# Splitting batch 0 of a Sinkhorn attention over both partition halves

## The chip, the cores and the metric

The kernel runs on one core of a Trainium2 chip. The metric is the device time of one execution in microseconds, as the median of three runs.

## The reference

Four batches, 8 heads, 768 positions, head size 64. The positions form 8 blocks of 96. A small matrix `sort_net` (8 x 8 for each batch and head) is normalised five times over rows and columns after an exponential, and its result P mixes the blocks of keys and values. Each block of queries then attends only to the mixed block of the same number. The result, 3072 tokens of 512, goes through a gated FFN of width 1536.

```python
P = sort_net
for _ in range(5):
    P = np.exp(P - np.max(P, axis=-1, keepdims=True))
    P = P / (np.sum(P, axis=-1, keepdims=True) + 1e-09)
    P = P / (np.sum(P, axis=-2, keepdims=True) + 1e-09)
k_sorted = np.einsum('bhij,bhjcd->bhicd', P, k_b)
v_sorted = np.einsum('bhij,bhjcd->bhicd', P, v_b)
scores = scale * np.matmul(q_b, k_sb.transpose(0, 1, 2, 4, 3))
attn = softmax(scores)                       # over the 96 keys of the block
x = np.matmul(attn, v_sb)                    # then tokens x (heads * 64)
g = x @ w_gate
out = (g / (1 + np.exp(-g)) * (x @ w_val)) @ w_out
```

## The kernel before

**Batches and units.** Every batch is split into 8 units. In the kernel before, a unit is four blocks of one pair of heads: `half, g = divmod(u, 4)`, heads 2g and 2g+1, blocks half*4 to half*4+3. A unit goes through scores (`scores`), the exponential on ScalarE (`exps`), the product with the mixed values (`av`: matmuls, then a reciprocal and a multiplication on VectorE into the tile `st`), and a transposition into `xt`, the FFN's input of 128 x 4 x 384. Four units fill one `xt`, which is one of eight FFN stages (`ffn(0)` to `ffn(7)`).

**The FFN.** `gate` and `value` are groups of four matmuls of 384 columns (L355, L373), followed by a tanh on ScalarE (L363) and two operations on VectorE (L365, L378). `outp` multiplies by the last weights (L390). `merge` lays the units of the next batch and its mixing between the FFN groups by fixed due times. From the first FFN stage on, TensorE and GpSimd run an order written out by hand, and the other engines follow.

**The opening.** Everything ahead of the first FFN stage is an order written by hand on TensorE, GpSimd, VectorE and ScalarE (`manual_schedule`). The parts are these.

- SyncE issues the load of `sort_net` into `p_sb` and nothing else until the first outputs. GpSimd's queue issues, in this order, two halves of v (batch 0), the identity, q, four pieces of k, then three transposing copies of v into `vch` (L124), a copy `landed` that waits for the last piece of k (L144), and the weights. The loads from GpSimd's queue cast fp32 to bf16 on the way.
- VectorE clears tiles (L70 to L163; L163 writes the column of ones of `vt`, 128 elements with a step of 65), then runs the five normalisations in turn with ScalarE's exponentials (L184 to L200). In iteration 1 it also makes the 0/1 `mask` (L187) and copies the identity into `rmix` (L188). The result is `p_bf` (L203).
- ScalarE makes four more copies of v into `vch` between its exponentials (L122).
- TensorE runs small matmuls on zeros (`dots`, `fill`, L420 and L416) in its gaps. Then it transposes P (`w_ps`, L432), and VectorE multiplies it by the mask into `rmix` (L439), a block-diagonal matrix over (head, block).
- Mixing: `v_chunk` multiplies pieces of `vch` (64 partitions) by `rmix` (L245), `kq_chunk` does the same for k and q together (L233). For this the tile `kq0` holds k on the lower 64 partitions and q on the upper 64, and `rmix` holds P below and the identity above, so that one matmul mixes k and transposes q. Each chunk is drained from PSUM by VectorE (L211) or ScalarE (L213).
- The first four units (`qk`, `av`, `x_to`) follow, with the first three FFN groups (`early`, L497) laid in where their inputs are ready. PSUM has two pairs of banks (tags a and b), three single banks (gen) and one more (x).

Of the kernel before, what the change touches and what calls it, by code (L numbers as in the profile page):

```python
# [9 lines left out]
FP32 = mybir.dt.float32  # L10
# [7 lines left out]
def kernel(  # L18
# [59 lines left out]
    e_all = const.tile([C, 8, 4 * C + 32], BF16)  # L78
# [12 lines left out]
    def load_k(b, lo, hi):  # L91
        rows = highr if b else lowr
        nc.gpsimd.dma_start(out=kq_tile(b)[rows, lo:hi, :], in_=k_nat[b, :, lo:hi, :])
# [6 lines left out]
    def load_q(b, lo, hi):  # L100
        rows = lowr if b else highr
        nc.gpsimd.dma_start(out=kq_tile(b)[rows, lo:hi, :], in_=q_nat[b, :, lo:hi, :])
# [31 lines left out]
    load_v(0, 0, HC)  # L134
    load_v(0, HC, C)
    make_identity(nc, ident)
    load_q(0, 0, C)
    for lo, hi in ((0, 32), (32, 64), (64, 80), (80, 96)):
        load_k(0, lo, hi)
    copy_v(nc.gpsimd, 0, lowr, 0)  # L140
    copy_v(nc.gpsimd, 0, lowr, 3)
    copy_v(nc.gpsimd, 0, lowr, 5, 8, 40, D)
    landed = const.tile([R, 1], BF16)
    nc.gpsimd.tensor_copy(landed, kq_tiles[0][0:R, C - 1, D - 1:D])  # L144
    for m in range(0, 1024, 256):
        load_gv(m, m + 256)
    load_v(1, 0, C)
    for m in range(1024, DF, 256):
        load_gv(m, m + 256)
# [5 lines left out]
    for t in rmix.values():  # L155
        nc.vector.memset(t, 0.0)
# [3 lines left out]
    def vt_tile(pair):  # L160
        if pair not in vts:
            t = vtp.tile([C, 2, H * NB, D + 1], BF16, name=f"vt{pair}", tag="vt")
            nc.vector.memset(t[:, :, :, D:D + 1].rearrange("p u n e -> p (u n) e"), 1.0)  # L163
            vts[pair] = t
        return vts[pair]
# [4 lines left out]
    mask = const.tile([128, H], BF16)  # L170
    id4 = ident.rearrange("p (u h j) -> p h u j", u=2, h=H)
# [10 lines left out]
    p_ps = bank_tile("p_ps")[0:BH, 0:NB * NB].rearrange("p (i j) -> p i j", j=NB)  # L182
    for it in range(N_ITER):
        nc.scalar.activation(p_ps, p_sb if it == 0 else p_ps, AF.Exp)  # L184
        if it == 1:
            with nc.allow_low_precision("0/1 mask"):
                nc.vector.tensor_reduce(mask, id4, axis=AX.XY, op=ALU.add)  # L187
            nc.vector.tensor_copy(rmix[0][highr, 1].rearrange("p h i -> p (h i)"), ident[highr, highr])  # L188
        if it == 2:
            copy_v(nc.scalar, 0, lowr, 2, 8)  # L190
        if it == 3:
            copy_v(nc.scalar, 0, lowr, 3, 8)
        rowred = rowreds[it]
        nc.vector.reduce_sum(rowred[:, :, 0], p_ps, axis=AX.X)
        nc.vector.reciprocal(rowred, rowred)
        nc.vector.tensor_mul(p_ps, p_ps, rowred.to_broadcast([BH, NB, NB]))
        nc.vector.reduce_sum(colred[:, 0, :], p_ps.transpose([0, 2, 1]), axis=AX.X)
        nc.vector.reciprocal(colred, colred)
        if it < N_ITER - 1:
            nc.vector.tensor_mul(p_ps, p_ps, colred.to_broadcast([BH, NB, NB]))  # L200
    for lo in (0, NB // 2):
        part = slice(lo, lo + NB // 2)
        nc.vector.tensor_tensor(  # L203
            p_bf[:, part], p_ps[:, part].unsqueeze(2).to_broadcast([BH, NB // 2, H, NB]),
            colred.unsqueeze(1).to_broadcast([BH, NB // 2, H, NB]), op=ALU.mult)
    copy_v(nc.scalar, 0, lowr, 4, 8)
    copy_v(nc.scalar, 0, lowr, 5, 8, 0, 40)

# [6 lines left out]
    kqts = {}  # L215
# [22 lines left out]
    def v_chunk(b, at, n, eng, tag):  # L238
        rows = slice(0, 128) if b % 2 else lowr
        dst = vt_tile(b // 2)[:, b % 2]  # L240
# [8 lines left out]
    def v_pair_chunk(pair, at, n, eng, tag):  # L249
        dst = vt_tile(pair)[:, :, :, at:at + n]  # L250
# [8 lines left out]

    es, sts, xts = {}, {}, {}  # L260
    ecount = [0]

    def scores(b, u, tag):
        half, g = divmod(u, H2)
        k_sb, k_at, q_sb, q_at = ((kqts[b], 0, kqts[b], GI * C) if b < 2 else
                                  (kqts["p"], (b - 2) * GI * C, kqts["q"], (b - 2) * GI * C))
        if tag == "gen":
            wide = None
            pss = [bank_tile("qk"), bank_tile("qk")]
        else:  # L270
            wide = pair_tile("qk", tag).rearrange("p (two n) -> p two n", two=2)
            pss = [wide[:, 0], wide[:, 1]]
        for i4 in range(4):
            at = (g * NB + half * 4 + i4) * C
            for two in range(2):
                lo = two * D
                nc.tensor.matmul(pss[two][:, i4 * C:(i4 + 1) * C],  # L277
                                 lhsT=k_sb[lo:lo + D, k_at + at:k_at + at + 128],
                                 rhs=q_sb[lo:lo + D, q_at + at:q_at + at + C],
                                 start=True, stop=True)  # L280
        return wide, pss

    def exps(b, u, wide, pss):
        n = ecount[0] % 8
        ecount[0] += 2
        if wide is None:
            for two in range(2):
                nc.scalar.activation(e_all[:, n + two, 0:4 * C], pss[two][0:C, 0:4 * C], AF.Exp, scale=scale)
        else:
            nc.scalar.activation(e_all[:, n:n + 2, 0:4 * C], wide[0:C, :, 0:4 * C], AF.Exp, scale=scale)  # L290
        es[(b, u)] = [e_all[:, n, :], e_all[:, n + 1, :]]
# [4 lines left out]
    def av(b, u, tag="a"):  # L296
        half, g = divmod(u, H2)
        vt = vts[b // 2][:, b % 2].rearrange("p (h i) e -> p h i e", h=H)
        av_ps = pair_tile("av_ps", tag).rearrange("p (two n) -> p two n", two=2)
        o = av_ps[:, :, 0:4 * (D + 1)].rearrange("p two (i e) -> p two i e", e=D + 1)  # L300
        for two in range(2):
            e = es[(b, u)][two]
            for i4 in range(4):
                nc.tensor.matmul(o[:, two, i4, :], lhsT=e[:, i4 * C:i4 * C + 128],  # L304
                                 rhs=vt[:, 2 * g + two, half * 4 + i4, :],
# [106 lines left out]
    idle_ps = bank_tile("idle_ps", "x")  # L412

    def fill(tile, n):
        for _ in range(n):
            nc.tensor.matmul(tile, lhsT=warm_sb[:, 0:128], rhs=warm_sb, start=True, stop=True)  # L416

    def dots(n):
        for _ in range(n):
            nc.tensor.matmul(idle_ps[0:32, 0:32], lhsT=warm_sb[:, 0:32], rhs=warm_sb[:, 0:32],  # L420
                             start=True, stop=True)

    dots(124)
    for it, n in ((1, 3), (2, 4), (3, 4), (4, 4)):
        nc.tensor.matmul(idle_ps[0:NB, 0:NB], lhsT=rowreds[it][:, :, 0], rhs=rowreds[it][:, :, 0],
                         start=True, stop=True)
        fill(idle_ps, n)

    def weights(half):
        w_ps = bank_tile(f"w_ps{half}")[:, 0:NB * B * H].rearrange("p (i b h) -> p i b h", b=B, h=H)  # L430
        for i in range(NB):
            nc.tensor.matmul(w_ps[half * R:(half + 1) * R, i].rearrange("p b h -> p (b h)"),  # L432
                             lhsT=p_bf[:, i].rearrange("p a b -> p (a b)"),
                             rhs=ident[0:BH, 0:BH], start=True, stop=True)
        return w_ps

    def mix_of(dst, b, w):
        lo = (b % 2) * R
        nc.vector.tensor_tensor(dst, mask[lo:lo + R].unsqueeze(2).to_broadcast([R, H, NB]),  # L439
                                w[lo:lo + R].transpose([0, 2, 1]), op=ALU.mult)  # L440

    w_lo = weights(0)
    mix_of(rmix[0][lowr, 0], 0, w_lo[:, :, 0])
    w_hi = weights(1)
    w_sb = const.tile([128, NB, 2, H], FP32)
    nc.scalar.copy(w_sb[lowr, :, 1], w_lo[lowr, :, 2])
# [182 lines left out]
```

## Time and profile before

| | us |
|---|---|
| span of the profiled execution | 248.0 |
| median of the three runs | 249.75 (249.3 to 249.91) |
| TensorE busy | 240.1 |
| VectorE busy | 157.7 |
| ScalarE busy | 110.3 |
| GpSimd busy | 52.5 |

The page gives the span of the profiled execution, from its first to its last instruction; 1.75 us lie between it and the median of the runs. Busy time is the time in which an engine has an instruction at work; on TensorE matmuls overlap, so its rows may sum to more than the time that passes. In the timelines each line is a group of like instructions: start, time from the start of the first to the end of the last, engine, line, operation, tiles and shapes, and in brackets the idle time ahead of it and what ended it.

### The profile page before, as it was taken

The numbers are of one execution on the slowest core, as the hardware profiler recorded it, in microseconds if no ns is written. First come the engines' busy times: TensorE is split into PE (matmuls) and PEld (weight loads), VectorE is DVE, ScalarE is ACT, GpSimd is POOL, SyncE is SP. The second block draws the span as 40 slices with busy tenths as digits, with TensorE's granted clock in tenths as the row PEclk, the third lists the DMA queues.
The fourth block names the chain that finished last, engine by engine and source line by source line (L and its number), as shares of the span: only waits on it lengthen the run. The fifth ranks groups of instructions, "written<-read, shape, count | busy, mean of one in ns | idle before, by whom it ended". The sixth has DMA issues, their size and how long they took to land.

```text
span 248.0 us, 6193 instructions
## 1 busy us (share of the span) xinstructions
PE 240.1 (97%) x2636; PEld 141.3 (57%) x2636; DVE 157.7 (64%) x332; ACT 110.3 (44%) x187; POOL 52.5 (21%) x47
## 2 busy tenths in 40 slices
PE   7899999999999999999999999999999999999994
PEld 6376566666555556655555655565555555555543
DVE  6778689887555775857657646755764585446700
ACT  2977553453544444454642552354244334232311
POOL 7948459960059200000000000000000000000000
PEclk9999999999999999999999999999999999999999
DMA  5959999999999296010122121112111121100122
GB/s 101 211 95 166 215 189 228 194 226 211 221 170 192 53 210 164 3 42 3 45 54 52 57 62 34 44 42 78 32 42 45 39 57 55 42 22 24 42 81 88
DMA packets 39530, 24.38 MB, mean 98 GB/s; under 512 B 27728, under 2 KB 35664, under 8 KB 38992
## 3 DMA queue, kind: packets, MB, share of 16 engines
q0 software_dynamic: 21328, 14.16, 38.9%
q1 hardware_dynamic: 18176, 9.84, 14.1%
q8 instruction: 20, 0.33, 0.5%
q14 instruction: 6, 0.05, 0.1%
HBM read 28.32 MB, written 7.86 MB: 146 GB/s over the span
## 4 chain that ended last, share of the span: by engine, by line
PE 83%; DVE 7%; ACT 3%; issue 3%; DMA 2%; DVEq 0%; ACTq 0%; POOLq 0%
PE v_ps L373 23%; PE o_ps L390 23%; PE g_ps L355 22%; PE tkq L233 4%; PE av_ps L304 3%; PE qk L277 2%; DVE gs_sb L365 2%; DMA v<-in_v_dram 2%; DVE st L310 2%; PE tv L245 2%; PE idle_ps L416 1%; DVE h L378 1%; PE o_ps L406 1%; ACT th_sb L363 1%; PE x_ps L321 1%
## 5 line engine op out<-in xcount | busy, mean ns | idle before, releaser
L365 DVE SCALAR_TENSOR_TENSOR gs_sb<-th_sb,g_ps 128x384 bf16<-128x384 bf16 x96 | 52.8, 550 | 51.8 <-ACT th_sb L363 49.1
L373 PE MATMUL v_ps<-xt,wv_sb 128*128 128x384 bf16 x380 | 77.3, 326 | 0.7 <-DVE gs_sb L365 0.4
L355 PE MATMUL g_ps<-xt,wg_sb 128*128 128x384 bf16 x376 | 76.5, 326 | 0.0
L363 ACT ACTIVATE th_sb<-g_ps 128x384 bf16<-128x384 f32 x96 | 47.1, 490 | 56.0 <-PE g_ps L355 53.5
L390 PE MATMUL o_ps<-wo_sb,h 128*128 128x512 bf16 x276 | 64.0, 379 | 0.0
L378 DVE SCALAR_TENSOR_TENSOR h<-v_ps,gs_sb 128x384 bf16<-128x384 f32 x96 | 53.3, 556 | 6.6
L373 PEld LDWEIGHTS <-wv_sb 128*128 128x128 bf16 x380 | 35.4, 97 | 24.6 <-issue 2.3
L355 PEld LDWEIGHTS <-wg_sb 128*128 128x128 bf16 x376 | 34.6, 97 | 23.2 <-issue 0.3
L390 PEld LDWEIGHTS <-h 128*128 128x128 bf16 x276 | 26.3, 98 | 28.9
L395 ACT COPY o_sb<-o_ps 128x512 f32<-128x512 f32 x23 | 13.5, 585 | 50.8 <-PE o_ps L390 50.8
L124 POOL COPY vch<-v 64x1536 bf16<-64x1536 bf16 (+2 forms) x11 | 28.6, 2639 | 20.7 <-DMA v<-in_v_dram 20.7
L290 ACT ACTIVATE e_all<-qk 96x768 bf16<-96x768 f32 x30 | 22.6, 802 | 8.1 <-PE qk L277 8.1
L310 DVE TENSOR_TENSOR st<-av_ps,r_sb 96x512 bf16<-96x512 f32 x32 | 21.7, 679 | 0.2
L304 PEld LDWEIGHTS <-e_all 96*128 96x128 bf16 x256 | 12.2, 98 | 4.9 <-ACT e_all L290 0.8
L304 PE MATMUL av_ps<-vt,e_all 96*128 96x65 bf16 x256 | 13.5, 194 | 0.0
L211 DVE CAST vt<-tv 96x1024 bf16<-96x1024 f32 (+1 forms) x9 | 9.8, 1100 | 2.7 <-PE tv L255 1.6
L308 DVE RECIPROCAL r_sb<-av_ps 96x8 f32<-96x8 f32 x32 | 6.4, 199 | 7.6 <-PE av_ps L304 7.5
L213 ACT CAST vt<-tv 96x1024 bf16<-96x1024 f32 (+1 forms) x9 | 9.2, 1032 | 3.1 <-PE tv L255 1.8
L211 DVE CAST kqt<-tkq 128x1024 bf16<-128x1024 f32 (+1 forms) x7 | 7.5, 1068 | 2.7 <-PE tkq L233 2.6
L213 ACT CAST kqt<-tkq 128x1024 bf16<-128x1024 f32 (+1 forms) x7 | 6.0, 894 | 6.6 <-PE tkq L233 6.6
L416 PE MATMUL idle_ps<-warm_sb 128*128 128x512 bf16 x28 | 8.7, 409 | 0.0
L233 PE MATMUL tkq<-rmix,kq 128*64 128x64 bf16 x384 | 7.8, 197 | 0.6 <-issue 0.6
(74 smaller groups left out, 126.3 us busy)
## 6 DMA issues: line engine op xcount, KB each, us to landing
out_dram<-o_sb SPq DMA_DIRECT2D x23, 256.0 KB, 2.0
v<-in_v_dram POOLq DMA_DIRECT2D x3, 768.0 KB, 19.9
kq<-in_q_dram POOLq DMA_DIRECT2D x2, 768.0 KB, 13.6
wg_sb<-in_moe_w_gate_dram POOLq DMA_DIRECT2D x6, 256.0 KB, 8.5
wv_sb<-in_moe_w_val_dram POOLq DMA_DIRECT2D x6, 256.0 KB, 9.1
wo_sb<-in_moe_w_out_dram POOLq DMA_DIRECT2D x1, 1536.0 KB, 23.8
kp<-in_k_dram POOLq DMA_DIRECT2D x2, 768.0 KB, 15.1
q_scr<-in_q_dram POOLq DMA_DIRECT2D x2, 768.0 KB, 29.9
```

Of the source, the lines that this page charges most:

```text
L124: eng.tensor_copy(dst, src.transpose([0, 2, 1]))
L211: nc.vector.tensor_copy(dst, src)
L233: nc.tensor.matmul(tp[two * D:(two + 1) * D, lc, :], lhsT=kq_tiles[b][:, at + lc, :], rhs=rm[:, two], start=True, stop=True)
L290: nc.scalar.activation(e_all[:, n:n + 2, 0:4 * C], wide[0:C, :, 0:4 * C], AF.Exp, scale=scale)
L304: nc.tensor.matmul(o[:, two, i4, :], lhsT=e[:, i4 * C:i4 * C + 128], rhs=vt[:, 2 * g + two, half * 4 + i4, :], start=True, stop=True)
L310: nc.vector.tensor_tensor(st.rearrange("p i two d -> p two i d"), o[0:C, :, :, 0:D], r_sb.to_broadcast([C, 2, 4, D]), op=ALU.mult)
L355: nc.tensor.matmul(g_ps, lhsT=wg_sb[:, kc, ts(m, 128)], rhs=xt[:, kc, :], start=(kc == 0), stop=(kc == NKC - 1))
L363: nc.scalar.activation(th_sb, g_ps, AF.Tanh, scale=0.5)
L365: nc.vector.scalar_tensor_tensor(gs_sb, th_sb, 1.0, g_ps, op0=ALU.add, op1=ALU.mult)
L373: nc.tensor.matmul(v_ps, lhsT=wv_sb[:, kc, ts(m, 128)], rhs=xt[:, kc, :], start=(kc == 0), stop=(kc == NKC - 1))
L378: nc.vector.scalar_tensor_tensor(h_tiles[n][:, m, :], v_ps, 0.5, gs_tiles.pop(m), op0=ALU.mult, op1=ALU.mult)
L390: nc.tensor.matmul(o_ps, lhsT=h_w[:, m, ts(t3, 128)], rhs=wo_sb[:, m, :], start=(m == 0), stop=(m == NFC - 1))
```

## The change

It touches the opening and, for the units of batch 0, the shapes.

- Values of batch 0 are loaded by SyncE in four pieces, as fp32, into a tile `v0` whose lower 64 partitions hold positions 0 to 47 of each block and whose upper 64 hold positions 48 to 95. Four transposing copies over 128 partitions (three on GpSimd, one on ScalarE) cast them into `vch0`.
- q and k of batch 0 are split over the partition halves in the same way, in the tile `qk0`: four loads of q, then six of k, all from GpSimd's queue. q is transposed by matmuls of its own (`q0_chunk`) against the identity; half of them run between the fourth and the fifth normalisation, the rest after the first value chunk. k is mixed by `k0_chunk`, values by `v0_chunk`, whose two halves take 64 partitions each.
- The mixed keys lie in `kqt0` with 128 columns for a block (two times 48 and 16 of zeros), so scores, exponentials and `av` of batch 0 work on 128 keys of which 32 are padding. The padding of `vt` has zeros, in the column of ones too; that column is written by five memsets for the two pairs of batches.
- `rmix[0]` is made by one operation over 128 partitions; the mask is made in iteration 2 and has 16 columns; the copy of the identity into `rmix[0]` is gone. The operations that make `rmix` of the other batches move from ahead of the first scores to behind `av` of unit 1.
- `landed` is gone. Memsets of padding on GpSimd are new.
- The first four units of batch 0 are two blocks of four heads each; `x_first` writes half of the columns of two parts of `xt`, and `early` runs the first three FFN groups in two halves of 192 columns, the first half after two units.
- Several `fill` calls are gone or moved.

```diff
-    load_v(0, 0, HC)
-    load_v(0, HC, C)
+    v0 = vnp.tile([128, HC, D], FP32, name="v0", tag="vn")
+    for lo, hi in ((0, 24), (24, HC)):
+        for a, rows in enumerate(halves):
+            nc.sync.dma_start(out=v0[rows, lo:hi, :], in_=v_nat[0, :, a * HC + lo:a * HC + hi, :])
+    load_qk0(0, q_nat, 0, 24)
+    load_qk0(0, q_nat, 24, HC)
     make_identity(nc, ident)
-    load_q(0, 0, C)
-    for lo, hi in ((0, 32), (32, 64), (64, 80), (80, 96)):
-        load_k(0, lo, hi)
-    copy_v(nc.gpsimd, 0, lowr, 0)
-    copy_v(nc.gpsimd, 0, lowr, 3)
-    copy_v(nc.gpsimd, 0, lowr, 5, 8, 40, D)
-    landed = const.tile([R, 1], BF16)
-    nc.gpsimd.tensor_copy(landed, kq_tiles[0][0:R, C - 1, D - 1:D])
+    nc.gpsimd.memset(vch0[:, :, HC:], 0.0)
+    load_qk0(1, k_nat, 0, 16)
+    load_qk0(1, k_nat, 16, 32)
+    load_qk0(1, k_nat, 32, HC)
+    copy_v0(nc.gpsimd, 0, 24, 32, D)
+    copy_v0(nc.gpsimd, 24, HC, 0, 32)
+    copy_v0(nc.gpsimd, 24, HC, 32, D)
+    nc.gpsimd.memset(kqt0[:, 0:NK].rearrange("p (n c) -> p n c", c=D)[:, :, HC:], 0.0)
     for m in range(0, 1024, 256):
         load_gv(m, m + 256)
     load_v(1, 0, C)
+    nc.gpsimd.memset(vch[lowr, D * D:D * C], 0.0)
...
-            nc.vector.memset(t[:, :, :, D:D + 1].rearrange("p u n e -> p (u n) e"), 1.0)
+            if pair == 0:
+                nc.vector.memset(ones[:, 0], 0.0)
+                for lo in (0, R):
+                    nc.vector.memset(ones[lo:lo + HC, 0], 1.0)
+                nc.vector.memset(ones[0:C, 1], 1.0)
+            else:
+                nc.vector.memset(ones[0:C], 1.0)
...
+    def q0_chunk(at, n, tag):
+        dst = kqt0[:, NK:].rearrange("p (n a c) -> p a n c", a=2, c=HC)
+        sel = ident.rearrange("p (a g two j) -> p two (a g) j", a=2, g=H2, two=2)
+        tp = chunk_tile("tq0", n // 8, tag).rearrange("p (l n) -> p l n", n=2 * GI)
+        for lc in range(n):
+            for two in range(2):
+                nc.tensor.matmul(tp[two * D:(two + 1) * D, lc, :], lhsT=qk0[:, 0, at + lc, :],
+                                 rhs=sel[:, two], start=True, stop=True)
+        return dst[:, :, :, at:at + n], tp.rearrange("p l (a n) -> p a n l", a=2)
+    def v0_chunk(at, n, eng, tag):
+        tp = chunk_tile("tv0", n // 8, tag).rearrange("p (l n) -> p l n", n=H * NB)
+        for ld in range(n):
+            for a, rows in enumerate(halves):
+                nc.tensor.matmul(tp[rows, ld, :], lhsT=vch0[rows, at + ld, :],
+                                 rhs=rmix[0][rows, a].rearrange("p h i -> p (h i)"),
+                                 start=True, stop=True)
+        drain(eng, vts[0][:, 0, :, at:at + n], tp.transpose([0, 2, 1]))
...
-            nc.vector.tensor_copy(rmix[0][highr, 1].rearrange("p h i -> p (h i)"), ident[highr, highr])
+        if it == 3:
+            copy_v0(nc.scalar, 0, 24, 0, 32)
+        if it == N_ITER - 2:
+            early_q = [q0_chunk(0, 16, "b"), q0_chunk(16, 8, "gen")]
+        if it == N_ITER - 1:
+            for dst, src in early_q:
+                drain("s", dst, src)
...
+    v0_chunk(0, 16, "v", "a")
+    q_late = [q0_chunk(24 + 8 * n, 8, "gen") for n in range(3)]
+    for dst, src in q_late:
+        drain("s", dst, src)
+    v0_chunk(16, 16, "v", "b")
+    nc.scalar.copy(w_sb[lowr, :, 1], w_ps[lowr, :, 2])
+    nc.scalar.copy(w_sb[highr], w_ps[highr].rearrange("p i (pair u) h -> p i pair u h", u=2)[:, :, :, 1])
+    k0_chunk(0, 8, "s", "gen")
+    k0_chunk(8, 8, "s", "gen")
+    v0_chunk(32, 16, "v", "a")
+    v0_chunk(48, 16, "s", "b")
+    k0_chunk(16, 8, "s", "gen")
+    k0_chunk(24, 8, "v", "gen")
+    k0_chunk(32, 8, "s", "gen")
+    k0_chunk(40, 8, "v", "gen")
+    fill(idle_ps, 3)
     qk(0, 0, "a")
     qk(0, 1, "b")
     qk(0, 2, "gen")
     fill(idle_ps, 2)
     av(0, 0, "a")
     fill(idle_ps, 2)
     av(0, 1, "b")
+    for b in range(1, B):
+        mix_of(...)
+    x_first(0, "s", "x")
+    qk(0, 3, "a")
+    av(0, 2, "b")
+    x_first(1, "s", "gen")
+    early(0, range(NKC), 0)
+    av(0, 3, "a")
+    early(1, range(NKC), 0)
+    x_first(2, "s", "x")
+    early(2, range(NKC), 0)
+    x_first(3, "v", "x")
+    for n in range(3):
+        early(n, range(NKC), 1)
```

## The prediction

> **What bounds the kernel now.** I read the page first (engine totals, the slices), then the timelines of the first 30 us engine by engine, because the change touches nothing later.
>
> ```profile
> span 248.0 us, 6193 instructions
> PE 240.1 (97%) x2636; PEld 141.3 (57%) x2636; DVE 157.7 (64%) x332; ACT 110.3 (44%) x187; POOL 52.5 (21%) x47
> PE 83%; DVE 7%; ACT 3%; issue 3%; DMA 2%; DVEq 0%; ACTq 0%; POOLq 0%
> ```
>
> TensorE is busy for 97% of the span and carries 83% of the chain of waits: from the first full FFN matmul on, the kernel is a stream of matmuls. A change of the opening moves the end by as much as it moves the start of that stream. I call the start F. The TensorE timeline gives four marks:
>
> ```profile
> 12.30 2.04 PE L245 MATMUL tv<-rmix,vch 64*128 64x64 bf16 x64
> 14.27 2.16 PE L233 MATMUL tkq<-rmix,kq 128*64 128x64 bf16 x112
> 20.24 0.69 PE L277 MATMUL qk<-kqt 64*128 64x96 bf16 x24
> 27.24 0.81 PE L373 MATMUL v_ps<-xt,wv_sb 128*128 128x384 bf16 x4
> ```
>
> T = 12.30, block mixing starts; Q = 20.24, first scores; F = 27.24. So mixing takes 7.94 us and the first units 7.00 us. What stands ahead of T is seen on VectorE and GpSimd:
>
> ```profile
> 1.94 0.17 DVE L163 MEMSET vt<- 96x128 bf16 x1 [0.41 <-issue]
> 2.51 0.17 DVE L163 MEMSET vt<- 96x128 bf16 x1 [0.41 <-issue]
> 2.65 0.21 DVE L194 TENSOR_REDUCE rowred<-p_ps 32x8 f32<-32x64 f32 x1
> 4.26 0.32 DVE L188 COPY rmix<-ident 64x64 bf16<-64x64 bf16 x1
> 4.61 0.21 DVE L194 TENSOR_REDUCE rowred<-p_ps 32x8 f32<-32x64 f32 x1
> ```
> ```profile
> 1.27 1.19 POOL L108 DMA_DIRECT2D v<-in_v_dram  x2 [0.82 <-POOLq L613]
> 6.30 6.18 POOL L124 COPY vch<-v 64x1536 bf16<-64x1536 bf16 x3 [0.70 <-DMA v<-in_v_dram]
> 15.94 0.18 POOL L144 COPY landed<-kq 64x1 bf16<-64x1 bf16 x1 [3.45 <-DMA kq<-in_k_dram]
> ```
>
> Each strided memset of vt comes after 0.41 us in which VectorE stands still for no semaphore. The two v issues on GpSimd take 652 and 547 ns, so they end at about 1.92 and 2.46, just before the memsets at 1.94 and 2.51 start. I read that as the memset being held until a descriptor issue ends. Values land at 6.25 and k at 15.94; T waits for neither, only for the normalisation.
>
> **The change, part by part.**
>
> *Normalisation (ahead of T).* The rmix COPY goes and the mask reduction moves to iteration 2. The exp of iteration 1 ended at 4.28, its reduction began at 4.61, elsewhere 0.03 after the exp: gain 0.30 us. Against it stand five strided vt memsets for two, beside four q issues in a row on GpSimd (about 1.27 to 3.5 at 0.53 to 0.65 each). If none is held, they take 384 elements at 0.17 us per 128, end by 2.0 and cost nothing, as the first exp ends at 2.62. If one goes into each gap (1.94, 2.51, 3.03, 3.55, 3.62), the first reduction starts at 3.75, 1.1 us late. The short ones have half the elements and may pass in twos, which gives 3.25. I take 0.9, near the case that the rows show. Sum for this path: +0.6, T at 12.9.
>
> The Trainium skill, "VectorE: DVE Perf Modes", section "Zero memsets can be issued as uint32 (trn2)", says that a memset takes one cycle per element. By that alone the five cost nothing here and T would be 12.0; the start-to-start distance of the two rows, 0.57 us for 128 elements, contradicts it, and the row decides.
>
> *Values (ahead of T).* They leave the GpSimd queue for SyncE's, four issues behind the one for sort_net (0.40 us each by that row: 0.75 to 2.75; that queue has nothing else to issue before the outputs at 62.9), and land as fp32, beside q on the other queue. Between 4 and 14 us the windows show 182 to 242 GB/s written as bf16, so about 200 written and 400 read. v and q are 3.15 MB to read and now 2.36 MB to write. If reading limits: 3.15/0.4 = 7.9 us from 2.2, v whole at 10.1. If writing into a 64-partition half limits: 2.36/0.2 = 11.8 us, v whole at 14.0. No row shows a plain fp32 load into half of the partitions; I take the middle, 12.0. Then GpSimd's second copy must run (768 elements for 1536: from the rows of 653 ns for 288 and 2829 for 1536, 1.74 ns an element plus 0.15, so 1.5 us), since the first value chunk reads it: T at 13.5, between 11.6 and 15.5. It is later than 12.9 and decides: T +1.2. ScalarE's one copy (1.5 us by its 64x768 rows) sits ahead of the last exp, where 1.5 us are free; it costs nothing if the first v quarters land by 8.
>
> The Trainium skill, "DMA: Bandwidth & Descriptors", section "Rules for kernel authors", speaks against the split: two transfers to the two partition halves serialize, one over 128 partitions is better. "SBUF — State Buffer", section "Door 1: The DMA port swizzle (why `[64,N]` ≈ `[32,N]`)", gives 196 GB/s for 64 partitions; estimated from it, v's 1.57 MB alone take 8.0 us. Read-limited loads would leave T at 12.9, serialized halves put it at 15.5.
>
> *GpSimd's queue.* The last k third (two issues, about 1.1 us) now waits for q's first quarters; behind it stand three value copies, a pad memset and all weight loads. The k and q pad memsets (1024 elements each; ident's 128 took 0.25) cost about 1.3 each. Weights start at 13.5 + 1.5 + 1.3 = 16.3 instead of 16.06. Nothing: the first weight is read at 25.0. That cover of 5 us gone, each us is a us of F. k moves after q and v: 1.57 MB at 400 GB/s from 12.0 is whole at 16, and its last third is read 4.5 after T, at 18.0; no wait. The vch memset later (2048 elements, 2.5 us) stands behind eight queued loads and costs nothing.
>
> *Mixing, T to Q.* The 24 early q rows leave this stretch (48 of 192 matmuls at 18 ns and 1536 of 10240 drained elements), and so do three fills of 0.32 and the 0.57 us issue gap, while the values' matmuls double to 128. TensorE needs 2.3 + 0.9 + 1.7 = 4.9 us and no longer sets the pace; the drains do. By this kernel's rows (DVE 1024 elements 1.22, 512 0.68; ACT 1.06 and 0.60) ScalarE has 3 q drains, w_sb twice, 4 k and 1 v: 5.4 us starting 0.95 after T. The last k chunk waits for a bank until 5.75, is multiplied at 6.15 and drained at 6.85. So 6.9 for 7.94: gain 1.0, between 0.6 and 1.5.
>
> *First units, Q to F.* As before, VectorE ends st of unit 0 at Q+2.64 and of unit 1 at Q+3.48. Then the three mix rows (0.26 + 0.54), which lay beside the wait for Q, stand in its queue and unit 2's reciprocal waits behind them: to 4.28, st done at 5.2. Unit 3's scores wait for unit 0's bank, its exp ends on ScalarE at 4.3 and x_first(1)'s drain behind it at 4.75; TensorE in order then does half of early(0), av(0,3) at 4.97, reciprocal 5.43, st 6.36, transposes 6.4 to 6.74, drain 7.13, and ten matmuls of 192 columns at 0.08: F = Q+8.0. Before it was 7.0. Half-width FFN work fills waits, but the last st is 1.05 later (25.55 is Q+5.31). Cost +1.0, between +0.4 and +1.2.
>
> Sum: +1.2 − 1.0 + 1.0 = +1.2 on F. The page gives a span of 248.0 and the runs a median of 249.75; I keep the 1.75 between them. Predicted: 250.9 us.
>
> **The rivals.**
>
> *Faster.* Loads are limited by what is read. Then v is whole at 10.1, its copies end at 11.6 and T goes with the normalisation, at 12.0 if the memsets pass freely. With mixing at 6.4 and a tail of 7.4, F = 25.8 to 26.4: about −1.1, 248.6. For it: 365 GB/s written in the half microsecond at 7.0, when v and q fill both halves. It decides if v lands before 10.5 and the first reduction starts by 2.9.
>
> *Cancelled.* The same loads but held memsets: T at 12.7, mixing 6.9, tail 7.8, F = 27.4: 249.9.
>
> *Much slower.* Writes to one half at a time limit: v whole at 14.0, T at 15.5, Q 22.4, F = 30.1 to 30.4: +2.9, 252.7. For it: the steady 200 GB/s written into one half. It decides from a landing after 13.
>
> **How the numbers follow.** Forecast 0.40, faster 0.28, cancelled 0.14, much slower 0.18. About 0.3%, 0.75 us, is what this measurement can tell. Of the forecast's 0.40, 0.07 lies within that, as a v landing 0.4 us earlier brings it there. So faster 0.28, same 0.21, slower 0.51. The range runs from 248.4 (the faster case, a little further) to 252.7, leaving out the tails beyond both. The forecast's own range is 250.2 to 251.8.
>
> **What would show it.** Right: vt memsets spread to 3 us and beyond; the first tv0 matmul waiting for GpSimd's copy, near 13.5; the last k drain 6.9 after it; three mix rows between st of units 1 and 2; the first L452 row near 28.4. Wrong: v landed by 10, T near 12, or L452 before 27.

## The result and the profile after

The changed kernel takes 261.27 us (median of 4 runs, 258.64 to 261.33) against 249.83 us before (249.3 to 249.93). The ratio is 1.0423, with a 95% interval of 1.0371 to 1.0475. The prediction of 250.9 us and its range up to 252.7 us are both missed; the sign of the forecast is right, its size is not. The profiled execution took 261.33 us, 1.77 us more than its span.

The same lines of the page as before:

```profile
span 259.6 us, 6353 instructions
PE 243.4 (94%) x2706; PEld 144.3 (56%) x2706; DVE 156.8 (60%) x331; ACT 107.3 (41%) x187; POOL 55.6 (21%) x52
...
PEclk9988799999999999999999999999999999999999
...
PE 79%; DVE 6%; DMA 5%; issue 3%; ACT 3%; SPq 1%; POOL 1%; DVEq 0%; ACTq 0%; POOLq 0%
```

TensorE is busy for 3.3 us more in a span 11.6 us longer, so most of the loss is standing still. DMA now has 5% of the chain (2% before), and the granted clock, which was at its full value in every slice before, dips in slices 3 to 5. TensorE's timeline gives the three marks and two stops:

```profile
17.42 1.06 PE L284 MATMUL tv<-rmix,vch 64*64 64x64 bf16 x32 [2.46 <-POOL vch L157]
24.53 0.32 PE L276 MATMUL tk<-rmix,qk 128*64 128x64 bf16 x9 [0.74 <-ACT kqt L213]
26.86 0.29 PE L276 MATMUL tk<-rmix,qk 128*64 128x64 bf16 x7 [2.01 <-issue]
28.03 1.14 PE L356 MATMUL qk<-kqt 64*128 64x96 bf16 x24
37.05 0.81 PE L452 MATMUL v_ps<-xt,wv_sb 128*128 128x384 bf16 x4
```

T is 17.42, Q is 28.03, F is 37.05. T waits for GpSimd's value copy, as forecast, but four microseconds later. In the middle of the last key chunk TensorE stops for 2.01 us with no semaphore to wait for ("issue"). The sum by stretches, in us:

| stretch | before | after | difference | predicted difference |
|---|---|---|---|---|
| start to T | 12.30 | 17.42 | +5.12 | +1.2 |
| T to Q | 7.94 | 10.61 | +2.67 | −1.0 |
| Q to F | 7.00 | 9.02 | +2.02 | +1.0 |
| F to the end of the span | 220.76 | 222.51 | +1.75 | 0 |
| span | 248.00 | 259.56 | +11.56 | +1.2 |

What holds T is read on GpSimd and ScalarE:

```profile
10.22 0.51 POOL L142 DMA_DIRECT2D qk<-in_k_dram  x1 [2.08 <-DMA qk<-in_q_dram]
...
15.89 2.91 POOL L157 CAST vch<-v 128x768 bf16<-128x768 f32 x2 [3.35 <-DMA v<-in_v_dram]
...
19.62 0.80 POOL L110 DMA_DIRECT2D wg_sb<-in_moe_w_gate_dram  x1
```
```profile
11.01 1.51 ACT L155 CAST vch<-v 128x768 bf16<-128x768 f32 x1 [2.73 <-DMA v<-in_v_dram]
12.43 0.20 ACT L303 ACTIVATE p_ps<-p_ps 32x64 f32<-32x64 f32 x1
```

The four value quarters landed at 7.62, 10.93, 13.40 and 15.77, in step with q's on the other queue (7.34, 9.94, 12.66, 15.36). ScalarE's copy of the first two quarters stands ahead of the last exp and waits for them for 2.73 us, so the normalisation too ends late, at 14.60. On VectorE the vt memsets, and the first reduction behind them:

```profile
2.42 0.11 DVE L188 MEMSET vt<- 48x64 bf16 x1 [0.27 <-issue]
2.81 0.11 DVE L189 MEMSET vt<- 96x64 bf16 x1 [0.27 <-issue]
3.12 0.37 DVE L311 TENSOR_REDUCE rowred<-p_ps 32x8 f32<-32x64 f32 x1 [0.20 <-issue]
```

Last, the windows from 14 us on (stretch, length, busy time and count of PE, PEld, DVE, ACT and POOL, granted TensorE clock, DMA share, GB/s):

```profile
16.00:18.00 2.00, 0.58 (x22) 0.59 (x24) 0.00 (x0) 0.00 (x0) 2.00 (x2) 0.85 0.88 161
18.00:20.00 2.00, 2.00 (x72) 1.87 (x70) 1.23 (x1) 0.91 (x2) 2.00 (x3) 0.50 0.09 15
20.00:22.00 2.00, 2.00 (x96) 1.90 (x95) 1.06 (x1) 1.70 (x6) 2.00 (x4) 0.80 0.41 39
...
28.00:30.00 2.00, 2.00 (x28) 1.31 (x28) 0.00 (x0) 1.44 (x3) 2.00 (x3) 0.50 1.45 195
```

Each stop of TensorE of over 2 us (before 17.42 and before 26.86) is followed by 3.4 us at half clock: the trace has 0.50 from 17.39 to 20.80 and from 27.63 to 31.04, and these windows average over it. The Trainium skill, "TensorE: Matmul & The Clock Gate", section "HAM oscillation — how this bites in real kernels", describes a clock that falls back during waits above about 3.4 us; here waits of 2.46 and 2.01 us were enough, and the measurement decides.

### The profile page after: what moved, and what is told of

Same layout as the page of the kernel before. It is cut to its first block, busy times and chain, and to the rows that moved or that the text cites. A ratio compares the mean times of both kernels' runs of the same rounds, so it can differ in the third digit from the quotient of the medians.

```text
span 259.6 us, 6353 instructions
## 1 busy us (share of the span) xinstructions
PE 243.4 (94%) x2706; PEld 144.3 (56%) x2706; DVE 156.8 (60%) x331; ACT 107.3 (41%) x187; POOL 55.6 (21%) x52
## 4 chain that ended last, share of the span: by engine, by line
PE 79%; DVE 6%; DMA 5%; issue 3%; ACT 3%; SPq 1%; POOL 1%; DVEq 0%; ACTq 0%; POOLq 0%
PE v_ps L452 22%; PE o_ps L469 22%; PE g_ps L434 21%; DMA v<-in_v_dram 5%; PE av_ps L383 3%; PE tkq L233 3%; PE qk L356 2%; DVE gs_sb L444 2%; DVE vt L211 1%; DVE st L389 1%; DVE h L457 1%; PE tv L284 1%; PE o_ps L485 1%; PE idle_ps L293 1%; ACT th_sb L442 1%
## 5 line engine op out<-in xcount | busy, mean ns | idle before, releaser
L370 ACT ACTIVATE e_all<-qk 96x768 bf16<-96x768 f32 (+1 forms) x31 | 23.4, 804 | 11.2 <-PE qk L356 11.2
L123 POOL COPY vch<-v 64x1536 bf16<-64x1536 bf16 (+1 forms) x8 | 22.4, 2853 | 17.6 <-PE g_ps L434 15.7
L383 PEld LDWEIGHTS <-e_all 96*128 96x128 bf16 (+1 forms) x256 | 12.6, 99 | 5.4 <-ACT xt L213 0.6
L211 DVE CAST vt<-tv 96x1024 bf16<-96x1024 f32 (+1 forms) x9 | 11.0, 1220 | 6.5 <-PE tv L284 4.4
L383 PE MATMUL av_ps<-vt,e_all 96*128 96x65 bf16 (+1 forms) x256 | 13.7, 195 | 0.4 <-DVE st L389 0.4
L213 ACT CAST vt<-tv 96x1024 bf16<-96x1024 f32 (+1 forms) x7 | 7.9, 1133 | 3.1 <-PE tv L255 1.8
L284 PE MATMUL tv<-rmix,vch 64*64 64x64 bf16 x128 | 3.5, 216 | 2.5 <-POOL vch L157 2.5
L419 POOL DMA_DIRECT2D q_scr<-in_q_dram x2 | 5.7, 3232 | 0.0
## 6 DMA issues: line engine op xcount, KB each, us to landing
wv_sb<-in_moe_w_val_dram POOLq DMA_DIRECT2D x6, 256.0 KB, 10.1
```

Source lines behind the costliest of these rows:

```text
L123: eng.tensor_copy(dst, src.transpose([0, 2, 1]))
L211: nc.vector.tensor_copy(dst, src)
L370: nc.scalar.activation(e_all[0:keys, n:n + 2, 0:4 * C], wide[0:keys, :, 0:4 * C], AF.Exp, scale=scale)
L383: nc.tensor.matmul(o[:, two, n, :], lhsT=e[:, n * C:n * C + 128], rhs=vt[:, 2 * g + two, i, :], start=True, stop=True)
```

## The experiments

All kernels are edits of the changed kernel unless said otherwise, and one profiled execution of each is read. As the four runs of the changed kernel spread over 2.7 us, differences of a microsecond or two rest on the marks in the traces, not on the times. The kernel before, run once beside the first four of these kernels, took 252.25 us there, and 249.76 beside the next six. "T to Q" and "Q to F" are differences between the rows of the three marks.

**The order of the halves.**

```
-        for a, rows in enumerate(halves):
+        for a, rows in ((1, highr), (0, lowr)):
             nc.sync.dma_start(out=v0[rows, lo:hi, :], in_=v_nat[0, :, a * HC + lo:a * HC + hi, :])
```

> Only the order of the four value loads is turned round: of each pair the upper partition half is loaded first, while q's loads on the other queue still begin with the lower half. Theory A (the two queues run in step and write into the same 64 partitions at the same time, and that half is what limits): v and q now write into opposite halves, so together they go well above the 203 to 237 GB/s of the windows; the last value quarter lands near 11.5 instead of 15.77, the first mixing matmul T comes near 13.5 instead of 17.42, and the time falls by about 4 us, to 257. Theory B (bytes written limit wherever they go, and fp32 values are twice the bytes): the last quarter still lands near 15.8, T stays near 17.4 and the time at 261.

259.02 us. The DMA windows and the first mixing matmul:

```profile
4.00:8.00 4.00, 2.81 (x34) 1.33 (x32) 3.24 (x16) 0.37 (x2) 3.54 (x7) 1.00 1.07 283
8.00:12.00 4.00, 3.84 (x60) 1.73 (x59) 2.46 (x13) 2.28 (x4) 2.01 (x2) 1.00 1.03 267
15.71 0.69 PE L284 MATMUL tv<-rmix,vch 64*64 64x64 bf16 x32 [2.54 <-POOL vch L157]
```

The same two windows of the changed kernel hold 228 and 217 GB/s. Two queues that write opposite halves get more, as theory A says, and a value packet of 6144 bytes takes 284 ns (median) instead of 441. But the last quarter lands at 14.07, 1.7 us earlier and not 4: v and q still advance in step, so v is whole only when both are. A is right on the half and wrong on how much it is worth.

**One transfer over both halves.**

```
-        for a, rows in enumerate(halves):
-            nc.sync.dma_start(out=v0[rows, lo:hi, :], in_=v_nat[0, :, a * HC + lo:a * HC + hi, :])
+        nc.sync.dma_start(out=v0[:, lo:hi, :],
+            in_=v_nat[0].rearrange("r (a c) d -> a r c d", a=2)[:, :, lo:hi, :])
```

and the same for q and k on GpSimd.

> Each pair of half loads of batch 0 (values on SyncE's queue, q and k on GpSimd's) becomes one load over all 128 partitions; tiles, types and everything after stay. Theory A (half of the partitions limits): all values have landed by about 11, T near 13, time 256 to 257; with half as many issues GpSimd's queue also moves on about 2.5 us earlier. Theory B (bytes written limit): the last values land near 15.5, T near 17, time 260 to 261.

292.34 us, which neither theory expected. TensorE stands still for 25.5 us ahead of its first query matmul, waiting for q. A window of that time:

```profile
24.00:28.00 4.00, 0.00 (x0) 0.00 (x0) 0.00 (x0) 0.00 (x0) 0.00 (x0) 0.50 0.13 39
```

A DMA share of 0.13 is 2 of 16 engines. The Trainium skill, "DMA: Bandwidth & Descriptors", section "Rules for kernel authors", says that an outermost dimension of a size under 16 confines a transfer to that many engines; the outermost dimension here is the two halves, and the trace agrees. So the run says nothing on the two theories, except this: with only two engines at work, a value packet of 6144 bytes takes 247 ns. The 441 ns of the changed kernel are therefore not the packet's own length: they come from the crowd of 16 engines, and, by the run before, above all from their writing into one half.

**Values by GpSimd, as bf16.**

```
-    v0 = vnp.tile([128, HC, D], FP32, name="v0", tag="vn")
+    v0 = vnp.tile([128, HC, D], BF16, name="v0", tag="vn")
-            nc.sync.dma_start(out=v0[rows, lo:hi, :], ...)
+            nc.gpsimd.dma_start(out=v0[rows, lo:hi, :], ...)
```

> Undoes only 'values fp32 by SyncE': the four value loads are issued by GpSimd ahead of q's, cast to bf16 into a bf16 tile; the split over both halves and all else stay. Both theories of the loads expect values whole near 7.5 (before: 6.25 by two loads) and T with the normalisation, at 12.9 to 13.3. What it tells apart is what came after T: if the longer mixing (10.6 us) and first units (9.2) follow from the late T (dropped clock, code and weight loads meeting), they fall to about 7 and 8, F is near 28.5 and the time 250 to 251.5; if they belong to the new arrangement itself, they stay, F is near 33 and the time 256 to 257.

257.57 us. The quarters land at 4.95, 6.24, 9.03 and 9.69; T is 15.20, not 13:

```profile
12.22 4.37 POOL L157 COPY vch<-v 128x768 bf16<-128x768 bf16 x3
15.20 0.69 PE L284 MATMUL tv<-rmix,vch 64*64 64x64 bf16 x32 [1.24 <-POOL vch L157]
```

The values are there at 9.69, but GpSimd's copies stand behind its last two key issues, which wait for q to land, and start at 12.22. The early query chunk (ahead of the weights' transposes on TensorE) waits for q as well, until 11.57. So T has three locks, one behind the other: v's landing, the copies' place in GpSimd's queue, and q. After T there are two stops without a semaphore, of 1.05 us ending at 18.97 and of 2.35 us ending at 24.68; the next runs explain them. T to Q is 10.65 and Q to F 9.17, as long as in the changed kernel, so the late T alone is not what lengthened them. The span ends 1.32 us after the last output transfer, as before (1.27), where the changed kernel needs 2.06.

**Fills in the gap.**

```
+    idle_ps = bank_tile("idle_ps", "gen")
+    fill(idle_ps, 7)
     v0_chunk(0, 16, "v", "a")
```

> Seven matmuls of zeros (512 columns) are put between the weights' transposes and the first value chunk, so that TensorE does not stand still for the 2.46 us in which it waits for GpSimd's copy. Clock theory: the granted clock (0.85, 0.50 and 0.80 in the windows from 16 to 22 us) stays at 1.0 there, T is unchanged at 17.4, mixing takes 8.5 to 9.5 us instead of 10.6 and the time falls by 1 to 2 us. Rival (the drains and the 2.0 us issue gap pace the mixing, not the clock): mixing stays at 10.3 to 10.7 and the time within 0.5 us of 261.3.

256.23 us, more than the clock theory hoped for:

```profile
23.23 0.78 PE L276 MATMUL tk<-rmix,qk 128*64 128x64 bf16 x16 [0.74 <-ACT kqt L213]
24.88 0.69 PE L356 MATMUL qk<-kqt 64*128 64x96 bf16 x24
32.88 0.81 PE L452 MATMUL v_ps<-xt,wv_sb 128*128 128x384 bf16 x4
18.00:20.00 2.00, 2.00 (x116) 1.90 (x112) 1.60 (x2) 1.50 (x4) 2.00 (x3) 1.00 0.02 3
```

T is unchanged at 17.40, the clock stays at 1.00, and F comes 4.17 us earlier: T to Q is 7.48, Q to F 8.00. Seven useless matmuls removed not only the slow clock but also nearly all of the 2.01 us stop, which I had not expected (about 0.3 us is left inside the first row above, where a matmul that starts at 23.23 is followed by one at 23.59). That pointed to the trace's instruction reads (queue q8, 16 KB each). Counted in the trace (matmuls, weight loads and waits), TensorE's stops without a semaphore in the opening fall at its 704th and 960th instruction, to within two, and so 256 apart, in every kernel that has them. The kernel before has one too, at the 704th:

```profile
17.60 0.54 PE L233 MATMUL tkq<-rmix,kq 128*64 128x64 bf16 x23 [0.57 <-issue]
```

In the changed kernel instruction 704 is passed at 21.23, the next read starts at 24.64, ends at 25.59, and TensorE goes on at 26.86. With the fills, which add 14 instructions to the count, the 704th is passed at 19.83 and the read starts at 20.95, just ahead of the weights: GpSimd issues them from 19.63 on, and their first packet moves at 21.14.

**Weights held back.**

```
+    nc.gpsimd.memset(vch[lowr, D * D:D * C], 0.0)
     for m in range(0, 1024, 256):
         load_gv(m, m + 256)
     load_v(1, 0, C)
-    nc.gpsimd.memset(vch[lowr, D * D:D * C], 0.0)
```

> GpSimd's memset of 1.9 us on the second part of vch moves ahead of the weight loads, so these start at 21.5 instead of 19.62; nothing else moves. Fetch theory: TensorE's next 16 KB of code were asked for near 20.6, when weights already filled the DMA engines, came through at 24.64 only, and TensorE stood still for 2.01 us in the last key chunk (mid chunk, no semaphore). With the weights later that fetch starts before 22, the 2.0 us go, mixing takes about 8.6 us instead of 10.6 (the clock still drops) and the time falls by about 2 us. Rival (the stop belongs to this place in the code, or to the dropped clock): a stop of 2 us stays in the last key chunk, mixing 10.4 to 10.7, time within 0.5 us of 261.3.

257.84 us, with T at 17.27:

```profile
24.37 0.44 PE L276 MATMUL tk<-rmix,qk 128*64 128x64 bf16 x16 [0.74 <-ACT kqt L213]
25.69 0.69 PE L356 MATMUL qk<-kqt 64*128 64x96 bf16 x24
33.69 0.81 PE L452 MATMUL v_ps<-xt,wv_sb 128*128 128x384 bf16 x4
```

The clock still falls after the wait for GpSimd (0.50 in 18 to 20), but the stop is gone: instruction 704 is passed at 21.09, the read starts at 21.85, and nothing waits. T to Q is 8.42, Q to F 8.00. So the fetch theory holds, and the parts separate. The slow clock costs mixing 8.42 − 7.20 = 1.2 us, where 7.20 is the kernel "units as before" below, which has full clock and no stop (the 7.48 above has 0.3 us of stop in it). The stop costs 10.61 − 8.42 = 2.2 us, and the half clock after the stop 9.02 − 8.00 = 1.0 us of the first units: in the six kernels with these units that have half clock there Q to F is 8.88 to 9.17, in the three that do not it is 8.00.

**Values first.** GpSimd's identity and pads ahead of q's issues:

```
+    make_identity(nc, ident)
+    nc.gpsimd.memset(vch0[:, :, HC:], 0.0)
+    nc.gpsimd.memset(kqt0[...key pads...], 0.0)
     load_qk0(0, q_nat, 0, 24)
     load_qk0(0, q_nat, 24, HC)
```

> GpSimd makes the identity and both pads (about 2.4 us) ahead of q's issues, so q starts near 3.6 instead of 1.28 and the first value loads of SyncE have the DMA engines to themselves. Theory A (both queues in one half at the same time are the loss; alone, an fp32 packet of 6144 B takes what a cast packet of 6144 B read takes, 0.25 us): the first two value quarters land by about 5 and 6 instead of 7.62 and 10.93, the last by 10 to 11, T is 12.5 to 13.5, time 256 to 257. Theory B (total bytes): the last quarter lands within 1 us of 15.8 again, T 16.5 to 17.5, since q's bytes only shift; time 260 to 261.

262.69 us. The value quarters land at 5.82, 7.56, 10.82 and 13.44, and q's first two only at 11.77 and 13.76. By the median of the 16 engines the first two are complete at 5.50 and 7.26, that is 1.76 us for 393 KB or 223 GB/s, with v alone (q's first packet moves at 7.06): theory A's "alone, an fp32 packet takes 0.25 us" is wrong (428 ns in the median). With the first experiment, bytes written into one half are what limits. T is 18.26, because TensorE, in order, now waits for q:

```profile
13.90 1.49 PE L266 MATMUL tq<-ident,qk 128*64 128x64 bf16 x48 [3.39 <-DMA qk<-in_q_dram]
```

The run also settles the vt memsets. GpSimd issues no DMA before 3.05 here, and in "values by GpSimd, as bf16" SyncE issues no values, and yet in both VectorE's rows are those of the changed kernel to a hundredth of a microsecond, such as this one:

```profile
2.42 0.11 DVE L188 MEMSET vt<- 48x64 bf16 x1 [0.27 <-issue]
```

**Units as before.** The kernel with fills, with the first units as four blocks of one pair, full-width FFN matmuls and the mix rows ahead of the first scores:

```
-        if b == 0 and half == 0:
-            return [(2 * (u % 2) + gg, 2 * (u // 2) + ii) for gg in range(2) for ii in range(2)]
```

> The kernel with seven fills ahead of the first value chunk, and in it the first units as before: four blocks of one pair of heads, 384-column FFN matmuls, the mix rows ahead of the first scores. My term of the prediction says that units of two blocks by four heads cost 1.0 us between first scores and first full FFN matmul (8.00 us with the fills): here 7.0 us, time about 255.2, 1 us under the kernel with fills. Rival (the units cost nothing, weights landing late set this stretch): 7.8 to 8.1 us and no change, 256.2.

255.73 us. Q to F is exactly 1.00 us shorter:

```profile
24.75 0.69 PE L354 MATMUL qk<-kqt 64*128 64x96 bf16 x24
31.75 0.81 PE L450 MATMUL v_ps<-xt,wv_sb 128*128 128x384 bf16 x4
```

T to Q is 7.20, and F comes 1.13 us earlier than in the kernel with fills. Of that 0.5 us reaches the span (254.0 for 254.5), mostly because TensorE stops for 0.47 us until 62.46, in a key chunk of batch 1, where the kernel with fills does not. How the 1.0 us divides among the blocks, the half-width matmuls and the place of the mix rows, this run does not separate.

**Values first, keys behind the copies, fills.** As "values first", with the last two key issues put behind two of GpSimd's copies and four fills:

```
     copy_v0(nc.gpsimd, 24, HC, 0, 32)
+    load_qk0(1, k_nat, 32, HC)
     copy_v0(nc.gpsimd, 24, HC, 32, D)
```

> Values first as in the run before, the last two key issues on GpSimd put behind two of its value copies, and four fills ahead of the first value chunk. If values' landing, the copies' place in GpSimd's queue, the dropped clock and the late code fetch are together what my prediction lacked, T is 12.6 to 13.2, mixing 7.0 to 7.6 and the first units 8.0: F 27.6 to 28.8 and 249.5 to 251.5 us, that is the time that was predicted. If something else costs, F stays above 30 and the time above 253.

261.99 us and F at 38.68, a miss that says little on the parts: the early queries still wait for q until 13.72, the weights' transposes behind them start at 17.10, T is 19.19. GpSimd now reaches the weights at 17.32, instruction 704 is passed at 21.65, its read starts 4.5 us later:

```profile
28.45 0.35 PE L276 MATMUL tk<-rmix,qk 128*64 128x64 bf16 x11 [3.17 <-issue]
```

**Everything rearranged.** Values by GpSimd as bf16 ahead of q; ScalarE takes both copies of the first 32 columns; GpSimd's two others stand ahead of the last key issues; the early query chunks come behind the weights' transposes; two vt memsets come later; the first units are as before; one key drain moves to VectorE; the vch memset stands ahead of the weights.

> All that the runs so far point to, in one kernel that keeps the split over both halves and the queries transposed apart: values by GpSimd cast to bf16 ahead of q, ScalarE takes both copies of the first 32 value columns, GpSimd's two copies stand ahead of the last key issues, the early query chunks come behind the weights' transposes, two of the vt memsets come after the mix weights, the first units are four blocks of one pair, one key drain goes from ScalarE to VectorE, and the weight loads wait for the vch memset. Theory (the loss is the sum of these places, not the split itself): p_bf done by 11.5, T at 12.4 to 12.9, mixing 7.0 to 7.5, first units 7.0, F 26.5 to 27.4, end 1.3 us after the last output: 248.8 to 250.0 us, level with the kernel before or just under it. Rival (the split itself costs, through twice the value matmuls and 128-row drains): mixing 8 to 9, F above 28 and time above 251.

256.15 us. T is 12.83, as expected, and then:

```profile
17.71 0.28 PE L276 MATMUL tk<-rmix,qk 128*64 128x64 bf16 x6 [1.87 <-issue]
23.60 0.29 PE L276 MATMUL tk<-rmix,qk 128*64 128x64 bf16 x7 [2.06 <-issue]
```

T to Q is 11.93 with both stops in it. With T early, instruction 448 is passed at 12.98, while key loads fill the DMA engines (read at 15.35), and 704 when the weights do (read at 21.26). Less the stops, mixing is 8.0, part of it at a slow clock (0.73 in 16 to 20). The rival's numbers came out (F is 32.94), but not its reason: most of what is lost against the expectation are the two stops, not the split's own matmuls and drains, as the last run confirms.

**fp32 in GpSimd's queue.**

```
-            nc.sync.dma_start(out=v0[rows, lo:hi, :], ...)
+            nc.gpsimd.dma_start(out=v0[rows, lo:hi, :], ...)
```

> The values stay fp32, but their four loads are issued by GpSimd ahead of q's, in the same queue, instead of by SyncE in its own. Bytes written into one half limit (about 222 GB/s): the value quarters land 1.8 us apart, the last by about 10 to 11 instead of 15.77 (9.69 as bf16), q's after them near 14, and the end comes 1.3 us after the last output instead of 2.06, as SyncE has no loads. Rival (fp32 loads are slow by themselves, whatever the queue): the last value quarter after 13. The first mixing matmul then waits for GpSimd's copies, which stand behind the last key issues, or for the early queries: T 15 to 17.5, time 257 to 260.

262.61 us. The quarters land at 5.88, 7.61, 9.38 and 11.77 (medians over the engines 1.8 us apart: 222 GB/s), q's from 12.56 to 14.97. So fp32 alone costs 2.1 us against bf16 in the same queue (9.69), and the separate queue, in which v shares with q, another 4.0 (15.77). T is 17.80 all the same, as the early queries now wait for q until 13.44.

**Rearranged, weights later.** The rearranged kernel with the vch memset done three times, ahead of the weights:

```
+    for _ in range(3):
         nc.gpsimd.memset(vch[lowr, D * D:D * C], 0.0)
```

> The rearranged kernel with its weight loads held back by two more GpSimd memsets (3.8 us: first issue at 19.3 instead of 15.54). Fetch theory: TensorE stops at every 256th instruction whose 16 KB of code have not come; the code behind instruction 960 is asked for when instruction 704 is passed (17.7) and came at 21.26, behind weights. Now that fetch starts within 1.2 us, the second stop (2.06 us in the last key chunk) goes, the clock stays at 1.0 in the first units, which take 7.0 us instead of 8.18; the first stop (1.87 us at 15.84, its fetch queued behind key loads) stays. Mixing 9.3 to 9.9 instead of 11.93, F 29.1 to 29.8, 250.9 to 251.6 us: 1% below the rearranged kernel's 256.15 or more, still not below the kernel before. Rival (weights coming later are missed at the start of the FFN): F or the stretch after it grows by what the stop gives back, 254 or more.

253.14 us (4 runs), ratio to before 1.0146, interval 1.0116 to 1.0177:

```profile
16.90 0.28 PE L277 MATMUL tk<-rmix,qk 128*64 128x64 bf16 x6 [1.05 <-issue]
20.69 0.29 PE L277 MATMUL tk<-rmix,qk 128*64 128x64 bf16 x7 [0.65 <-issue]
28.86 0.81 PE L448 MATMUL v_ps<-xt,wv_sb 128*128 128x384 bf16 x4
```

The second stop shrinks from 2.06 to 0.65, as its read starts 1.1 us after instruction 704 is passed at 16.90, and not 3.6; Q is 21.86, Q to F 7.00. The first stop, which I expected to stay at 1.87, shrinks to 1.05 as well; why its read came sooner I did not trace. T to Q is 9.01, and less the two stops 7.31, against 7.37 in the kernel before less its own stop: in this arrangement the split's mixing itself is not slower. The rest of the second stop stays: mixing runs through 256 instructions in 2.95 us, and a read that starts at once still takes about 1.1 + 1.2 + 1.45 us to its use. The profiled run took 252.75, 1.15 us above the 251.6 that I expected at most, although F came sooner than expected; a stop of 0.76 us until 60.36, at instruction 1984, that is 960 + 4·256, is part of it, and the rest I did not trace. No version that I ran beats the kernel before.

## Why the prediction was wrong, step by step

The 11.56 us by which the span grew are, added up: T 5.12, mixing −0.74 with full clock and no stop, the slow clock in it 1.2, the stop 2.2, the units 1.0, the half clock in them 1.0, and 1.75 after F. The forecast had 1.2, −1.0 and 1.0 for T, mixing and units, and nothing for the others.

*Values (the term that failed first).* The step "v whole at 12.0, the middle between 10.1 and 14.0" is mis-sized: it was 15.77. The write-limited end was the right mechanism (about 222 GB/s into one half for fp32, shown with v in one queue and alone), yet 14.0 was no bound. The sum held q's bytes, but not those of the keys, of which 0.22 MB had moved when v's last packet ended at 14.87. Nor did it hold the 0.9 us from that packet to the landing. The GpSimd copy then took 1.46 us (2.91 for two), as predicted, and T followed at 17.42. (The 6.25 that I read for the kernel before is the landing of v's first half; the second came at 8.07. Nothing rested on it.)

*ScalarE's copy.* "It costs nothing if the first v quarters land by 8" named the right condition; they landed at 10.93, and the last exp came at 12.43 (9.77 where the values landed early). It did not decide T, because the value copy was later still.

*Normalisation.* Predicted +0.9 for the memsets, held by GpSimd's issues. The first reduction came 0.47 late, and "values first" shows that GpSimd's issues have nothing to do with it: a strided memset of 64 elements takes 0.39 us from start to start, one of 128 took 0.57, whatever GpSimd does. Where the values came early (as bf16 by GpSimd), p_bf was ready at 11.93, for 11.56 before: +0.37, predicted +0.6.

*GpSimd's queue.* Weights at 16.3 became 19.62, since the last key issue waited for q until 10.22 and the copies for v. "Nothing, a cover of 5 us" looked only at who reads the weights. What they cost is who stands behind them in the DMA engines: TensorE's own code.

*Mixing.* Predicted 6.9 with drains as the pace. With the clock kept and no stop it is 7.20, a miss of 0.3. What the sum lacked is 1.2 for the clock after the wait at T, and 2.2 for the code that came late because the slow clock had passed instruction 704 only when the weights were flowing. I had seen the 0.57 us issue gap of the kernel before and booked it as a gain without asking what it was.

*First units.* Predicted Q to F 8.0: measured 8.00 in both kernels that keep the clock there (fills, weights held back), and 7.00 with the units as before. With the fills the three mix rows stand between the `st` of units 1 and 2, as forecast, and the `st` of units 2 and 3 end at Q+5.27 and Q+6.30 (5.2 and 6.36 by the forecast). The term of +1.0 is right, in size and path; the other 1.0 in the changed kernel is half clock behind the stop.

*The end.* I kept everything after F. It grew by 1.75: 0.79 at the very end, after the last output transfer (2.06 us for 1.27), which the kernels with SyncE's four value loads have (2.06 to 2.08), and the four with values by GpSimd do not (1.32 to 1.33); and 0.78 for one more stop, until 68.03, at instruction 1984, which is 960 + 4·256. The remaining 0.18 I did not trace.

Of the rivals, "much slower" had the mechanism (T decided by a landing after 13) and a price of +2.9; the true chain from that landing cost four times as much, because the wait on TensorE bought a slow clock and a late fetch behind it.

## What to carry to other kernels

A wait that you add on TensorE is not paid once: price what it does to the clock of the next microseconds (3.4 here), and to the moment at which the next piece of code is asked for, against what fills the DMA engines then. Where a stage consists of many tiny matmuls, count its instructions in blocks of 256 and look for idle time without a releaser at those counts; weights that "nobody needs yet" can stop the engine from there. And two loads that both must be whole should stand in one queue in the order of need: in two queues side by side, each is done only when both are.

## What the runs showed of the hardware

- TensorE stopped at its 704th and 960th instruction for 0.3 to 3.17 us, and at its 1984th for 0.44 to 0.78 us. The 16 KB read ahead of the 960th started 0.8 to 1.2 us after the 704th was passed in the four kernels that passed it over a microsecond ahead of the weights' first packet, and 1.7 to 4.5 us after it in the nine that passed it within 0.1 us of that packet or later. The read took 0.9 to 1.6 us, and TensorE went on 1.3 to 1.5 us after its end. It is not quite the passing that asks for it: in three kernels in which TensorE had just stood waiting, the read ahead of the 704th started from 1.1 us before to 0.1 us after the 448th was passed. That the read waits behind the weights in the DMA engines is inferred from these times and from the runs that moved the one against the other. The Trainium skill, "Runtime: NRT & Kernel Launch", section "Instruction fetch mechanics", has the 16 KB blocks of 256 instructions, and the trace agrees; it calls the crossing mostly hidden, and there the measured stops speak against it; of the two sizes that it gives for the room, 2048 instructions for TensorE and two blocks, the reads, each started one block ahead, fit the two blocks.
- 16 engines writing into one 64-partition half got about 222 GB/s for fp32 (223 in "values first", quarters 1.8 us apart in "fp32 in GpSimd's queue"); two queues writing opposite halves 267 to 283. An fp32 packet of 6144 bytes took 247 ns with two engines at work, 284 with the halves opposed, 436 to 441 with all at one half.
- TensorE's granted clock was 0.50 for 3.4 us after each of ten stops of 1.87 to 2.61 us, from 0 to 1.8 us after their end on, and for 3.4 to 10.2 us after waits of 3.2 to 3.8 us. It stayed at 1.00 after ones of 0.97 us (the kernel with fills), 1.05 us (the last kernel) and 1.59 us ("values by GpSimd, as bf16", its wait for q).
- A strided memset of bf16 on VectorE stands still for 0.17 to 0.29 us (64 elements) or 0.41 us (128 elements) ahead of its row, whether GpSimd or SyncE issues loads beside it or not.
- Four loads on SyncE's queue lengthened the end of the program, after its last output transfer, by about 0.75 us (2.06 to 2.08 us, against 1.27 to 1.33 in the kernels without them); the two of "one transfer over both halves" by half of that (1.67).
